# Scores and probabilities in joint runs of eight PSUM banks, and maxima that reach q by one transfer

## The chip, the cores and the metric

The kernel runs on one core of a Trainium2 chip. Five engines work side by side: PE (matmul), DVE (vector), ACT (activation), POOL (masks, some arithmetic) and SP, which issues the transfers. Matmul results land in eight PSUM banks of 128 partitions by 512 float32 columns; DVE and ACT read them out, and only then can a bank be written again. The metric is the device time of one execution in microseconds.

## The reference

A pre-norm transformer block over 2048 tokens of width 448: sliding-window attention with 16 heads of width 28 (each query sees itself and the 255 tokens before it), then a gated feed-forward of width 1792, each added to its input.

```python
q, k, v = qkv[0], qkv[1], qkv[2]
scores = jnp.einsum("bhqd,bhkd->bhqk", q, k) * (Dh ** -0.5)
mask = (idx[:, None] - idx[None, :] >= 0) & (idx[:, None] - idx[None, :] < W)
scores = jnp.where(mask[None, None], scores, -1e9)
p = _softmax(scores, axis=-1)
o = jnp.einsum("bhqk,bhkd->bhqd", p, v)
...
h = x + _A_ref(_layernorm(x, axis=-1), A_wqkv, A_wo)
h2 = h + _B_ref(_layernorm(h, axis=-1), B_w_gate, B_w_up, B_w_down)
```

`_B_ref` is `(gelu(x @ w_gate) * (x @ w_up)) @ w_down`.

## The kernel before

The kernel is a recorder and a planner. `block_kernel` calls `op` for each piece of work with an engine, an estimated duration, a key (the order wished for), the tokens it reads and writes and the PSUM banks it holds. `Lists.run` then lays all pieces out in one go with its own clock: for each engine it takes, among those that could start soonest, the one with the least key, picks banks for it through `allowed(kind)`, and emits its instructions. The result is a fixed order per engine. `TURN` is what the planner charges when PE changes its tile form (`mode`), `WAKE` what it charges for a signal between engines.

Attention is cut into 16 blocks `B`: four groups of four heads (`g = B % 4`) by four chunks of 512 queries (`c = B // 4`). In a block the queries are eight units of 64 and the keys of the window are units of 64 too. PE works in three tile forms here. Projections, values and the output product use the full 128 x 128 array (mode 0). Scores and probabilities use tiles of 32 rows by 64 columns (mode 3): `j` is the head and picks the 32 rows and the PSUM bank, `h` the half of the partitions. The value sums of `attend` use 64 x 32 (mode 2). The feed-forward uses halves of the array (mode 1).

The softmax goes in two passes. First the scores with queries along the partitions: DVE adds the mask and takes the maximum of each row (L783, an operation with a second small row that reads the result out). The maxima of a block are turned by DVE (L827), written to DRAM by four transfers (L829) and read back into the 29th row of q by one (L831). Second the products are made again with keys along the partitions, this time with 29 rows, so that the maximum is subtracted in the matmul; ACT takes the exponential into `pp` (L789), POOL zeroes what the mask excludes (L814), and `attend` multiplies with v (L882). A block has 16 score units for B under 4 and 20 after that, and as many probability units.

`scores_and_probs` makes one run of mode 3. It holds four banks, one for each `j`, and puts into each up to 512 columns: a score tile of a later block beside probabilities of an earlier one. So the two readers of a bank, DVE and ACT, take turns on it (`ser`). DVE throws the masked scores into `junk`, of which there are two, by `j % 2`. `stage(s)` lists the runs of a block: five for B from 4 on, four or three before.

The full-array work between the runs is q and k projection (`project_tile`, L659, copies to SBUF by ACT or DVE), values (`values`, L626) and the output product (`output`, L944, added to the residual by DVE, L947). `drain` brings the value sums out (ACT, then DVE L919 to L925 with POOL between).

## Time and profile before

| what | us |
|---|---|
| median of two runs | 712.58 |
| lowest and highest run | 711.46, 713.7 |
| the profiled execution | 712.76 |
| its span, first to last instruction | 710.9 |
| granted PE clock, mean | 0.995 |

The page gives each engine's busy time over the span. A busy PE is not a PE at its peak: the ends of matmuls are modelled, and a run that waits for a bank in its middle can still look busy. So the rows of the order of time are read by their starts: from the start of one stretch of a tile form to the start of the next is what the stretch held PE for. Each float32 matmul of modes 2 and 3 stands in the trace as two records. Names in rows are those of the program: `bank` is PSUM, `mt` the tile that holds mask and junk, `mx` the maxima, `pp` the probabilities.

### The profile page before, as it was taken

Reading aid. Unit: us, or ns where it says so; the run is one execution under the profiler, and the core shown is the slowest. Engines: PE = TensorE matmul, PEld = TensorE weight load, DVE = VectorE, ACT = ScalarE, POOL = GpSimd, SP = SyncE. Lnnn points to the kernel's source line nnn. Section 1 sums busy time; section 2 is a strip of 40 time slices with the busy share of each in tenths; the row PEclk is TensorE's granted clock in tenths of the full one; section 3 lists DMA queues with packets and bytes.
Section 4 is the critical chain, followed back from the end, with each engine's and each line's share of the span. In section 5 each row is a group of like instructions: output and inputs, shape, how many; then the busy total and the mean of one; then the engine's idle time right before and its main releaser. Section 6 shows DMA issues by size and latency. Waiting matters only on the chain. (4 is left out here: it accounts for less than half of the span.)

```text
span 710.9 us, 22675 instructions
## 1 busy us (share of the span) xinstructions
PE 692.3 (97%) x9106; PEld 566.4 (80%) x9106; DVE 535.9 (75%) x1409; ACT 361.0 (51%) x864; POOL 205.4 (29%) x430
## 2 busy tenths in 40 slices
PE   9999999999999989899999999999999999999997
PEld 7777667667776767576988897888888999999886
DVE  8977777877686668554997989975855888977744
ACT  5736536565455454455763547444434445545430
POOL 6334545564556345554020112000000110120000
PEclk9999999999999999899999999999999999999999
DMA  9211102022131226503745585424303564353102
GB/s 314 84 38 30 35 18 68 9 41 50 34 77 31 50 91 181 156 3 106 164 109 135 157 229 161 124 80 136 91 3 110 163 194 124 119 156 100 41 14 104
DMA packets 68744, 69.82 MB, mean 98 GB/s; under 512 B 44384, under 2 KB 56608, under 8 KB 68064
## 3 DMA queue, kind: packets, MB, share of 16 engines
q1 hardware_dynamic: 68496, 68.27, 34.5%
q8 instruction: 71, 1.16, 0.7%
q14 instruction: 33, 0.27, 0.1%
q10 hardware_dynamic: 144, 0.11, 0.0%
HBM read 58.95 MB, written 22.58 MB: 115 GB/s over the span
## 5 line engine op out<-in xcount | busy, mean ns | idle before, releaser
L783 DVE CUSTOM_DVE_ANT_0 mt<-bank,mt 128x320 bf16<-128x320 f32 (+4 forms) x288 | 122.8, 448 | 33.9 <-PE bank L773 18.5
L789 ACT ACTIVATE pp<-bank 128x192 f32<-128x192 f32 (+3 forms) x300 | 99.6, 390 | 75.7 <-PE bank L773 49.3
L1393 PE MATMUL bank<-xT,proj 64*128 64x512 f32 x645 | 120.1, 388 | 0.0
L814 POOL TENSOR_SCALAR_AFFINE_SELECT pp<-pp 64x256 f32<-64x256 f32 x240 | 96.3, 416 | 60.1 <-ACT pp L789 53.0
L1393 PE MATMUL bank<-xo,proj 64*128 64x512 f32 x456 | 97.3, 388 | 0.3 <-DVE e L1309 0.3
L659 PE MATMUL bank<-xT 128*128 128x512 f32 x308 | 83.8, 405 | 5.0 <-ACT pp L789 3.4
L1393 PEld LDWEIGHTS bank<-xT,proj 64*128 64x128 f32 x645 | 81.7, 184 | 7.7
L1469 PE MATMUL bank<-proj,gh 64*128 64x448 f32 x624 | 74.6, 362 | 0.4 <-DVE e L1309 0.4
L659 PEld LDWEIGHTS bank<-xT 128*128 128x128 f32 x308 | 55.1, 188 | 24.8 <-issue 7.9
L1469 PEld LDWEIGHTS bank<-proj,gh 64*128 64x128 f32 x624 | 62.6, 184 | 6.2 <-DVE e L1309 0.7
L1393 PEld LDWEIGHTS bank<-xo,proj 64*128 64x128 f32 x456 | 59.5, 184 | 6.9 <-DVE e L1309 0.7
L773 PE MATMUL bank<-q,k 29*64 29x128 f32 (+4 forms) x1888 | 61.3, 309 | 1.1 <-DVE mx L783 0.6
L773 PE MATMUL bank<-k,q 28*64 28x320 f32 (+4 forms) x1120 | 57.3, 410 | 0.7 <-ACT pp L789 0.6
L1393 PE MATMUL bank<-xT,w 64*128 64x512 f32 x276 | 53.5, 389 | 0.3 <-DVE raw L1405 0.3
L773 PEld LDWEIGHTS bank<-q,k 29*64 29x64 f32 x1888 | 40.6, 131 | 16.3 <-issue 3.2
L1393 PE MATMUL bank<-xo,w 64*128 64x512 f32 x240 | 49.4, 390 | 0.7 <-DVE raw L1405 0.6
L1488 DVE TENSOR_TENSOR hres<-bank,hres 128x448 f32<-128x448 f32 (+1 forms) x85 | 47.0, 610 | 1.0 <-PE bank L1469 1.0
L626 PE MATMUL bank<-proj,xT 128*128 128x448 f32 (+1 forms) x220 | 46.1, 339 | 0.1
L626 PEld LDWEIGHTS bank<-proj,xT 128*128 128x128 f32 x220 | 35.4, 189 | 7.7 <-issue 3.9
L882 PE MATMUL bank<-pp,v 64*29 64x128 f32 (+4 forms) x1888 | 40.7, 312 | 0.5 <-POOL pp L814 0.3
L882 PEld LDWEIGHTS bank<-pp,v 64*29 64x29 f32 x1888 | 34.2, 106 | 8.5 <-issue 3.7
L773 PEld LDWEIGHTS bank<-k,q 28*64 28x64 f32 x1120 | 23.1, 130 | 21.0 <-ACT pp L789 8.6
(195 smaller groups left out, 1278.6 us busy)
## 6 DMA issues: line engine op xcount, KB each, us to landing
gu<-in_gu_dram SPq DMA_DIRECT2D x18, 480.0 KB
proj<-gu SPq DMA_DIRECT2D x24, 288.0 KB
proj<-down SPq DMA_DIRECT2D x22, 224.0 KB
proj<-gu SPq DMA_DIRECT2D x24, 192.0 KB
hres<-in_x_dram SPq DMA_DIRECT2D x16, 224.0 KB
w<-gu SPq DMA_DIRECT2D x12, 288.0 KB
out_dram<-hres SPq DMA_DIRECT2D x15, 224.0 KB
xT<-xn SPq DMA_DIRECT2D x26, 128.0 KB
```

What stands on the lines that cost most here:

```text
L626: op("pe", mm(224 * n), 0.29 if n == 1 else 0.38, key + a / 16, lambda a=a, h=h, wb=wb, xb=xb: nc.tensor.matmul(bank[b.k][:, 0:224 * n], x ...
L659: op("pe", mm(512) + 0.002, 0.403, key, lambda a=a, h=h, wb=wb, xb=xb: nc.tensor.matmul(bank[b.k], wqk[m][:, h, wb, :], xT[:, xb, cc * 128 ...
L773: nc.tensor.matmul(bank[banks[j].k][dst, at:at + 64 * n], w, x, start=True, stop=True, tile_position=(32 * j, 64 * h), skip_group_check=True)
L783: nc.vector.tensor_tensor_reduce(junk[j % 2][hs, lo:320], bank[b.k][hs, o:o + n], mask[hs, lo:320], 1.0, -BIG, OP.add, OP.max, mx[u][hs, 4 ...
L789: op("act", 0.065 + G.w * 0.00088, 0.16 + G.w * 0.00088, key, lambda: nc.scalar.activation(pp[:, j, G.at:G.at + G.w], bank[b.k][:, o:o + G ...
L814: nc.gpsimd.affine_select(a, a, pattern=[[0, 4], [-cm, 64]], compare_op=op_, fill=0.0, base=0, channel_multiplier=cm)
L882: nc.tensor.matmul(bank[banks[h].k][32 * j:32 * j + DH + 1, 64 * lo:64 * hi], v[HALF[h], at_v(4 * c - 2 + kh // 2), 4 * g + j, :], pp[HALF ...
L1393: nc.tensor.matmul(bank[b.k], w, xarea(u.cp, xl, xs, side)[:, xk], start=p in (1, 2, 5) and not k and not t, stop=t == 2, tile_position=(6 ...
L1469: nc.tensor.matmul(bank[banks[q].k][:, 0:D], h[oh][0]()[HALF[x], q * 128:q * 128 + 128], d[wh][0]()[HALF[x]], start=not ph and not y and n ...
L1488: op("dve", 0.07 + w * 0.463 / D, 0.163 + w * 0.463 / D, key, lambda: nc.vector.tensor_tensor(hres[:, t, c0:c0 + w], bank[b.k][:, c0:c0 + ...
```

## The change

The score units of all blocks are laid end to end and cut into fills of eight (`filled`), 512 columns, and so are the probability units, with no regard to the borders of tiles or blocks. There are 38 fills of each. Excursion `e` makes the probabilities of fill `e - 4` in four banks and then, forced to follow at once (`then`), the scores of fill `e` in four others. So a run of mode 3 holds eight banks; the planner lets the last four come free late by the length of the first half (`soft`). From excursion 32 on the two halves are separate runs. A score tile may be cut at a bank: its maxima then come in two pieces, in columns 0 to 15 and 16 to 31 of `mx`, and DVE merges them (L877). The exponentials of a bank are one instruction (L853). `junk` is a single tile now; its second place and another hold the turned maxima, which DVE makes with four 32 x 32 transposes (L880), and four transfers bring them straight into q (L883). The planner charges more for a change of tile form (`TURN`), starts joint runs at least `GAP` apart, keeps value sums back for `AFTER` behind a run, takes them by a later key (`LAG_V`), and lets projections use all eight banks (`allowed`).

```diff
-LAG_V = 33.0
+LAG_V = 45.0
...
-TURN = (0.11, 0.11, 0.11, 0.11)
+TURN = (0.2, 0.2, 0.14, 0.16)
+HOLD = 0.3
+SPLIT = 32
+AFTER = 2.5
+GAP = 4.0
+LAG = 4
...
                     if not ks:
                         return None, None
-                    k = min(ks, key=lambda k: max(t, bank_free[k] + WAKE[e]))
-                    t = max(t, bank_free[k] + WAKE[e])
+                    late = o.soft if o.soft and i > 3 else 0
+                    k = min(ks, key=lambda k: max(t, bank_free[k] + WAKE[e] - late))
+                    t = max(t, bank_free[k] + WAKE[e] - late)
...
+            found, now = [], cand[e]
+            if e == "pe" and forced:
+                now = forced
+            elif e == "pe":
+                due = min((o.key for o in now if o.soft and max(o.ready, since + GAP) <= free["pe"] + HOLD), default=None)
+                if due is not None:
+                    now = [o for o in now if o.key <= due or all(b.k is not None for b in o.banks)]
+            for o in now:
                 t, got = start_of(e, o)
+                if t is not None and e == "pe" and o.mode == 2:
+                    t = max(t, since + AFTER)
...
-    junk = [mt[:, 192 + 192 * i:384 + 192 * i].bitcast(BF) for i in range(2)]
+    junk = mt[:, 192:352].bitcast(BF)
+    mxT = [mt[:, 352:480], mt[:, 576:704]]
...
+    def filled(items):
+        out, room = [[]], 8
+        for x, n in items:
+            a = 0
+            while a < n:
+                if not room:
+                    out.append([])
+                    room = 8
+                w = min(n - a, room)
+                out[-1].append((x, a, w, 8 - room))
+                a, room = a + w, room - w
+        return out
...
+    score_fills = filled([((B, i), max(tile_keys(B, i)[1])) for B in range(NB) for i in range(4)])
+    prob_fills = filled([((B, x), PIECES[x][4]) for B in range(NB) for x in
+                         ("ABdf" if B < 4 else "ABDFCE" if B % 2 == 0 else "CEABDF")])
+    final = {(B, i): (n, a) for n, fl in enumerate(score_fills) for (B, i), a, w, o in fl}
+    cut_tiles = {B: [i for i in range(4) if final[B, i][1]] for B in range(NB)}
+    scores_end = {B: final[B, 3][0] for B in range(NB)}
+    probs_end = {B: n for n, fl in enumerate(prob_fills) for (B, x), a, w, o in fl}
...
+        steps, new = [], []
+        if pf is not None:
+            work, reads, width, writes = [], [], 0, []
+            for (B, x), a, w, o in prob_fills[pf]:
+                reads += [("q", B % 4), *(("qx", B % 4, j) for j in range(4)), *k_toks(B, True)]
+                at = 512 * (pf % 4) + 64 * o
+                G = Group(B, [(piece_part(x, a, w), 0)], at)
+                groups.setdefault(B, []).append(G)
+                new.append(G)
+                writes += G.span(0, 64 * w)
+                ke, ko, ue, uo, n = piece_part(x, a, w)
+                for j in range(4):
+                    for h, kh, u in ((0, ke, ue), (1, ko, uo)):
+                        work += part(B, h, j, kh, u, n, 64 * o, True)
+                width = 64 * (o + w)
+            steps.append((work, reads, writes, width, [Bank("bin") for j in range(4)]))
...
+        ops = []
+        for n, (work, reads, writes, width, banks) in enumerate(steps):
+            held, rd, wr = banks, reads, writes
+            if not n and len(steps) > 1:
+                held, rd = banks + steps[1][4], reads + steps[1][1]
+            cost = width * 4 / 2400 + 0.012
+            ops.append(op("pe", cost, cost + 0.2, key, lambda work=work, banks=banks: run(work, banks), rd, wr, held, tag="bin", mode=3))
+        if len(ops) > 1:
+            L.open["whole"] = L.open.get("whole", 0) + 1
+            L.all.setdefault("whole", []).append(ops[0])
+            ops[0].then, ops[0].soft = ops[1], ops[0].cost
+        if sf is not None:
+            banks = steps[-1][4]
+            for j in range(4):
+                for (B, i), a, w, o in score_fills[sf]:
+                    most(key, B, i, a, w, o, j, banks[j])
+        if pf is not None:
+            width, banks = steps[0][3:]
+            for j in range(4):
+                probs(key, pf, width, j, banks[j])
+            for G in new:
+                select(G, key + 1)
...
-        def most(B, i, o, n, j, hs, b):
-            n, lo = 64 * n, 320 - 64 * n
-
-            def go():
-                u = B % 2
-                nc.vector.tensor_tensor_reduce(junk[j % 2][hs, lo:320], bank[b.k][hs, o:o + n], mask[hs, lo:320],
-                                               1.0, -BIG, OP.add, OP.max, mx[u][hs, 4 * j + i:4 * j + i + 1])
-            op("dve", 0.08 + n * 0.00104, 0.165 + n * 0.00106, key, go, ["mask"],
-               [("mx", B % 2, 4 * j + i, hs.start) if hs.stop - hs.start == 64 else ("mx", B % 2, 4 * j + i), *ser(b)], b, tag="most")
...
+    def most(key, B, i, a, w, o, j, b):
+        n, u = tile_keys(B, i)[1], B % 2
+        to = 4 * j + i + (16 if a else 0)
+        for h in (2,) if n[0] == n[1] else (0, 1):
+            full, hs = n[h % 2], HALF[h]
+            x = 64 * min(w, full - a)
+            lo = 320 - 64 * full + 64 * a
+
+            def go(hs=hs, x=x, lo=lo):
+                nc.vector.tensor_tensor_reduce(junk[hs, 0:x], bank[b.k][hs, 64 * o:64 * o + x], mask[hs, lo:lo + x],
+                                               1.0, -BIG, OP.add, OP.max, mx[u][hs, to:to + 1])
+            op("dve", 0.08 + x * 0.00104, 0.165 + x * 0.00106, key, go, ["mask"],
+               [("mx", u, to, h)] if h < 2 else [("mx", u, to)], b, tag="most")
...
+    def probs(key, pf, width, j, b):
+        at = 512 * (pf % 4)
+        op("act", 0.065 + width * 0.00088, 0.16 + width * 0.00088, key, lambda: nc.scalar.activation(
+            pp[:, j, at:at + width], bank[b.k][:, 0:width], AF.Exp, scale=SCALE), (), [span("pp", PW * j + at, width)], b, tag="exp")
...
-        op("dve", 0.1, 0.2, key, lambda: nc.vector.transpose(mxT[u], mx[u]), al, [("mxT", u)], port=True)
+        cuts = cut_tiles[B]
+        if cuts:
+            al += [("mx", u, 16 + 4 * j + i) for j in range(4) for i in cuts]
+            a, d = cuts[0], (cuts[1] - cuts[0] if len(cuts) > 1 else 1)
+            m2 = [mx[u][:, o:o + 16].rearrange("p (j i) -> p j i", i=4)[:, :, a:a + d * (len(cuts) - 1) + 1:d] for o in (0, 16)]
+            op("dve", 0.08, 0.165, key, lambda: nc.vector.tensor_tensor(m2[0], m2[0], m2[1], op=OP.max), al,
+               [("mx", u, 4 * j + i) for j in range(4) for i in cuts])
         for a in range(4):
-            dma(key, 2, lambda a=a: nc.sync.dma_start(mx_d[u][0:16, 32 * a:32 * a + 32], mxT[u][32 * a:32 * a + 16]), [("mxT", u)],
-                [("mxd", u, a)], cost=0.45)
-        dma(key, 8, lambda: nc.sync.dma_start(qT[g][DH:128:32], mx_d[u][0:16].rearrange("(j i) t -> j (i t)", i=4)),
-            [("mxd", u, a) for a in range(4)], [("qx", g)], cost=0.45)
+            op("dve", 0.07, 0.16, key, lambda a=a: nc.vector.transpose(mxT[u][0:32, 32 * a:32 * a + 32], mx[u][32 * a:32 * a + 32]),
+               al, [("mxT", u, a)], port=True)
+        for j in range(4):
+            dma(key, 4, lambda j=j: nc.sync.dma_start(
+                qT[g][32 * j + DH:32 * j + DH + 1].rearrange("p (i t) -> p i t", i=4), mxT[u][4 * j:4 * j + 4, None]),
+                [("mxT", u, a) for a in range(4)], [("qx", g, j)], cost=0.45)
...
+        last = scores_end[s] if s < NB else len(prob_fills) - 1 + LAG
+        while made_exc[0] <= last:
+            e = made_exc[0]
+            made_exc[0] += 1
+            sf, pf = e if e < len(score_fills) else None, e - LAG if LAG <= e < LAG + len(prob_fills) else None
+            key = 8 * e if e < 8 else 64 + 6.4 * (e - 8)
+            for x in ((sf, pf),) if e < SPLIT else ((None, pf), (sf, None)):
+                if x != (None, None):
+                    excursion(key, *x)
+            for B in range(NB):
+                if scores_end[B] == e:
+                    maxima(B)
+                if probs_end[B] == pf:
+                    collect(B)
...
         if kind in ("ln1", "v", "proj", "task"):
-            return [7, 6, 5, 4] + ([3, 2, 1, 0] if not left["bin"] or kind in ("v", "ln1") and L.fresh("bin") else [])
+            return [7, 6, 5, 4, 3, 2, 1, 0]
```

The fence below shows PE in the program before, behind a value sum: two runs with full-array work between. `k_158,q_162` are scores of one block, `q_165,k_161` probabilities of another; both go to the same four banks.

```order
L944 MATMUL bank_151<-wos,proj 128x448
L773 MATMUL bank_144<-k_158,q_162 64x320 x2
L773 MATMUL bank_145<-k_158,q_162 64x320 x2
L773 MATMUL bank_146<-k_158,q_162 64x320 x2
L773 MATMUL bank_149<-k_158,q_162 64x320 x2
L773 MATMUL bank_144<-q_165,k_161 64x192 x2
L773 MATMUL bank_145<-q_165,k_161 64x192 x2
L773 MATMUL bank_146<-q_165,k_161 64x192 x2
L773 MATMUL bank_149<-q_165,k_161 64x192 x2
L659 MATMUL bank_150<-xT 128x512 x3
L659 MATMUL bank_151<-xT 128x512 x6
```

And PE in the changed program, at the scores of block 7: the end of one run, one projection tile, and the first half of the next run. The names `k_157,q_161` are scores of block 7, `q_160,k_156` probabilities of block 6. Runs follow each other this closely in ten places.

```order
L784 MATMUL bank_145<-k_157,q_161 64x128 x2
L784 MATMUL bank_146<-k_157,q_161 64x128 x2
L784 MATMUL bank_147<-k_157,q_161 64x128 x2
L784 MATMUL bank_141<-k_157,q_161 64x128 x2
L680 MATMUL bank_140<-xT 128x512 x11
L784 MATMUL bank_142<-q_160,k_156 64x320 x2
L784 MATMUL bank_143<-q_160,k_156 64x320 x2
L784 MATMUL bank_144<-q_160,k_156 64x320 x2
L784 MATMUL bank_145<-q_160,k_156 64x320 x2
L784 MATMUL bank_142<-q_160,k_156 64x192 x2
L784 MATMUL bank_143<-q_160,k_156 64x192 x2
L784 MATMUL bank_144<-q_160,k_156 64x192 x2
```

Scores and probabilities no longer share a bank, and what stood as four banks of mixed work is eight banks of unmixed work; bank 145, written last by the first run, is wanted again in the next.

DVE before, two runs of scores one behind the other (`ISA mt,mx` is the reduction, `ISA mx` its read-out; the brackets name the engines that a row waits for):

```order
L783 ISA mt,mx_80<-bank_146,mt 128x320 [waits PE_49]
L783 ISA mx_80 128x1
L783 ISA mt,mx_80<-bank_150,mt 128x320 [waits DVE_49,PE_49]
L783 ISA mx_80 128x1
L783 ISA mt,mx_80<-bank_147,mt 128x320 [waits Activation_49]
L783 ISA mx_80 128x1
L783 ISA mt,mx_80<-bank_151,mt 128x320 [waits DVE_49,Activation_49]
L783 ISA mx_80 128x1
```

DVE in the changed program, the end of a run whose banks hold pieces of two blocks, and the maxima of the first of them:

```order
L846 ISA mt,mx_79<-bank_147,mt 128x256 [waits DVE_49,PE_49]
L846 ISA mx_79 128x1
L846 ISA mt,mx_80<-bank_147,mt 128x256 [waits DVE_49]
L846 ISA mx_80 128x1
L846 ISA mt,mx_79<-bank_140,mt 128x256 [waits DVE_49,PE_49,Activation_49]
L846 ISA mx_79 128x1
L846 ISA mt,mx_80<-bank_140,mt 128x256 [waits DVE_49]
L846 ISA mx_80 128x1
L877 TENSOR_TENSOR mx_79<-mx_79 128x8
L880 STREAM_TRANSPOSE mt<-mx_79 32x32 [waits DVE_49]
L880 STREAM_TRANSPOSE mt<-mx_79 32x32 x3
```

Every reduction here waits for an earlier DVE instruction, where every second one did; the waits for ACT on a shared bank are gone.

More of the change, by code (lines that the diff above doesn't have):

```diff
@@ L193, in start_of @@
             got = []
-            for b in o.banks:
+            for i, b in enumerate(o.banks):
                 if b.k is None:
@@ L260, in run @@
                 self.open[o.tag] -= 1
+            if o.then:
+                self.open["whole"] -= 1
             n -= 1
@@ L651, in project_tile @@
         main, extra = (("k", g, c % 2), ("kx", g, c % 2)) if s else (("q", g), ("qx", g))
+        more = [("qx", g, j) for j in range(4)] * (not s)
         B = 4 * c + g
@@ new lines, in excursion @@
+        if sf is not None:
+            work, reads, width = [], [], 0
+            for (B, i), a, w, o in score_fills[sf]:
+                g, c = block(B)
+                reads += [("q", g), *k_toks(B, False)]
+                lows, n = tile_keys(B, i)
+                for j in range(4):
+                    for h in range(2):
+                        work += part(B, h, j, lows[h] + a, 2 * i + h, min(w, n[h] - a), 64 * o, False)
+                width = 64 * (o + w)
+            steps.append((work, reads, [], width, [Bank("bin") for j in range(4)]))
@@ L1703, in block_kernel @@
             ln2(1)
-        make_groups(B)
         stage(B)
@@ L1750, in allowed @@
         if kind[0] == "gu0":
-            return [] if left["proj"] or left["v"] else [5 + kind[1]]
+            return [] if left["proj"] or left["v"] or left["whole"] else [5 + kind[1]]
         if kind[0] == "gu":
```

130 lines of the change are left out of this document (32 added, 98 removed).

## The prediction

> **What bounds the kernel now.** I read the page first, then the table of busy time by stretches, then the order of time on PE and DVE inside one stretch. The page says which engine has no room, the stretches say where the change can act.
>
> ```profile
> PE 692.3 (97%) x9106; PEld 566.4 (80%) x9106; DVE 535.9 (75%) x1409; ACT 361.0 (51%) x864; POOL 205.4 (29%) x430
> ...
> core 0: us, PE busy (x) PEld busy (x) DVE busy (x) ACT busy (x) POOL busy (x), PEclk, DMA share, GB/s
> 2.00:27.00 25.00, 24.66 (x142) 21.34 (x141) 22.23 (x54) 16.43 (x31) 14.96 (x37) 1.00 0.73 250
> 27.00:85.00 58.00, 56.21 (x849) 41.00 (x847) 46.62 (x220) 30.17 (x73) 21.89 (x45) 1.00 0.17 41
> 85.00:306.00 221.00, 213.50 (x4309) 154.05 (x4299) 162.21 (x534) 118.54 (x316) 116.85 (x264) 0.98 0.26 66
> 306.00:340.00 34.00, 32.85 (x534) 24.68 (x518) 16.31 (x31) 19.35 (x47) 15.72 (x37) 1.00 0.17 57
> 340.00:708.00 368.00, 364.65 (x3304) 325.05 (x3303) 287.58 (x570) 176.47 (x400) 34.70 (x43) 1.00 0.43 120
> ```
>
> Attention runs from 27 to 340 us; from 340 on PE does the feed-forward matmuls, busy 364.65 of 368 us, in the same number and tile forms before and after the change. So only the first 340 us can move. PE is the bound there, but its 97% hides three things: columns, changes of tile form, and short waits. The second engine matters: from 85 to 306 us, the twelve blocks 4 to 15, DVE is busy 162.21 of 221 us.
>
> **The price of leaving the full-array form.** These rows give it by differences.
>
> ```profile
> 27.41 0.79 PE L773 MATMUL bank<-k,q 28*64 28x320 f32 x16
> 28.13 2.60 PE L626 MATMUL bank<-proj,xT 128*128 128x224 f32 x21
> ...
> 178.28 2.81 PE L659 MATMUL bank<-xT 128*128 128x512 f32 x11
> 181.03 2.56 PE L882 MATMUL bank<-pp,v 64*29 64x192 f32 x128
> ...
> 238.38 0.73 PE L659 MATMUL bank<-xT 128*128 128x512 f32 x2
> 239.04 2.56 PE L882 MATMUL bank<-pp,v 64*29 64x192 f32 x128
> 241.53 0.79 PE L773 MATMUL bank<-k,q 28*64 28x320 f32 x16
> 242.12 0.53 PE L773 MATMUL bank<-q,k 29*64 29x192 f32 x16
> 242.58 0.50 PE L659 MATMUL bank<-xT 128*128 128x512 f32 x1
> ```
>
> A run of 16 x 320 = 5120 recorded columns holds PE 0.72 us (27.41 to 28.13), one of 8192 columns 1.05 us (241.53 to 242.58). 3072 more columns cost 0.33 us, so 5120 cost 0.55, and 0.17 to 0.18 us per run is left that is no column. In the same way two full-array matmuls hold PE 0.66 us, eleven 2.75: 0.23 each, and 0.20 per stretch that is none of them. A trip out and back costs 0.38 us.
>
> In the order of the two programs PE goes from 70 stretches of score form to 45, and from 74 full-array stretches to 55 (value sums keep 16): 25 x 0.18 + 19 x 0.20 = **8.3 us less**. This lies on PE, which sets the end, so nothing hides it.
>
> The columns are the same. The matmuls are cut otherwise: score form goes from 1504 to 1612 (two records each, so 216 more), value sums from 944 to 832 (224 records fewer).
>
> ```profile
> 153.80 1.20 PE L773 MATMUL bank<-q,k 29*64 29x128 f32 x48
> 154.93 1.42 PE L659 MATMUL bank<-xT 128*128 128x512 f32 x5
> ```
>
> These 8192 columns in 48 records take 1.13 us where 32 records took 1.05, 5 ns a record: +1.1 and -1.1, so 0, at worst 1 us either way.
>
> **What DVE gets in exchange.** A score tile that crosses a bank is reduced in two pieces: 400 reductions at L846 for 288 at L783. All of them now write one scratch tile, where two took turns. In the program 363 of the 400 wait for an earlier DVE instruction, of the 288 it was 152. What such a wait costs can be read here; the small row behind each reduction reads its result out.
>
> ```profile
> 187.10 0.49 DVE L783 CUSTOM_DVE_ANT_0 mt<-bank,mt 128x320 bf16<-128x320 f32 x1 [1.00 <-PE bank L773]
> 187.52 0.08 DVE L783 DVE_READ_ACCUMULATOR2_ANT mx<- 128x1 f32 x1
> 187.75 0.49 DVE L783 CUSTOM_DVE_ANT_0 mt<-bank,mt 128x320 bf16<-128x320 f32 x1
> 188.16 0.08 DVE L783 DVE_READ_ACCUMULATOR2_ANT mx<- 128x1 f32 x1
> 188.16 0.48 DVE L783 CUSTOM_DVE_ANT_0 mt<-bank,mt 128x320 bf16<-128x320 f32 x1
> ...
> 191.70 0.08 DVE L783 DVE_READ_ACCUMULATOR2_ANT mx<- 128x1 f32 x1
> 191.82 0.21 DVE L827 STREAM_TRANSPOSE mxT<-mx 128x32 f32<-128x32 f32 x1
> ...
> L783 DVE CUSTOM_DVE_ANT_0 mt<-bank,mt 128x320 bf16<-128x320 f32 x224 | 104.0, 484 | 28.2 <-PE bank L773 13.9 <-ACT pp L789 1.0 <-DVE mx L783 1.0
> L783 DVE CUSTOM_DVE_ANT_0 mt<-bank,mt 64x64 bf16<-64x64 f32 x16 | 3.3, 215 | 5.0 <-PE bank L773 4.6 <-ACT pp L789 0.2
> ```
>
> The reduction at 188.16 has no such wait and starts together with the read-out before it, 0.41 us behind its forerunner. The one at 187.75 waits for its own engine and for another one, and starts 0.65 behind: 0.23 lost. The transpose at 191.82 waits for its own engine alone and starts 0.04 after the read-out has ended instead of together with it: 0.12 lost. By width a column costs (484 - 215) / 256 = 1.05 ns, and 0.08 us is fixed.
>
> A bank of 512 score columns comes in 2.4 pieces on average: 0.54 + 2.4 x 0.08 + 0.23 (its first piece also waits for PE) + 1.4 x 0.12 = 1.13 us, 4.5 us for the four banks of a run. A block of blocks 4 to 15 is two and a half runs, 11.3 us. Before it was 16 reductions at 0.41 plus 0.23 for 58% of them, 8.7 us. Four small transposes for one and a merge of split maxima cost 0.1 to 1.0 us a block (the 0.21 row above is the nearest, the pieces are a quarter of it; I take 0.3), and copies of q and k that go from DVE to ACT give 0.25 back. So DVE gains 2.6 us of work per block, 31 us between 85 and 306. Its free time there is 221 - 162 = 59 us, less 0.14 us behind some 110 read-outs that no row counts as busy: 43. It is left with 12 us, and fewer if PE is to be faster.
>
> **What this does to PE.** Before, a run that stood directly behind another already waited for banks:
>
> ```profile
> 185.98 0.79 PE L773 MATMUL bank<-k,q 28*64 28x320 f32 x16
> 186.57 0.53 PE L773 MATMUL bank<-q,k 29*64 29x192 f32 x16
> 186.89 0.74 PE L773 MATMUL bank<-k,q 28*64 28x320 f32 x16
> 187.43 1.02 PE L773 MATMUL bank<-q,k 29*64 29x192 f32 x20
> 188.66 0.48 PE L773 MATMUL bank<-q,k 29*64 29x128 f32 x8 [0.21 <-ACT pp L789]
> 189.73 1.10 PE L773 MATMUL bank<-q,k 29*64 29x128 f32 x36 [0.58 <-DVE mx L783]
> 190.76 0.47 PE L944 MATMUL bank<-proj,ohl 128*128 128x448 f32 x1
> ```
>
> Its 24576 columns need 2.6 + 0.2 us and took 4.78: 2.0 lost. The same subtraction over all stretches from 27 to 340 leaves 29 us of waits, 12 of them in the seven stretches of this kind.
>
> After, a run takes all eight banks. Walk one that is followed by one projection tile of 11 matmuls, as in the order shown above. The run starts at 0, its scores are there at 2.0. PE reaches the next run at 2.0 + 2.75 = 4.75 and its score half at 5.6. ACT has emptied the probabilities long before,
>
> ```profile
> 287.05 2.06 ACT L789 ACTIVATE pp<-bank 128x512 f32<-128x512 f32 x4 [0.53 <-PE bank L773]
> ```
>
> four banks in 2.06 us. But DVE empties the score banks at 3.2, 4.4, 5.7 and 6.9, and the score half needs the last of them for its first eight matmuls: 1.35 us lost. Ten gaps are this short: 13.5 us. One run stands directly behind another: some 4 us. In the 18 longer gaps DVE has 6 to 12 us and I put 0.2 us each, 3.5. Together 21 us in place of 12: **9 us more**. The bounds: nothing (or the 12 us saved) if DVE keeps up, 38 us if each of the 28 joint runs loses 1.35.
>
> **The rest.** The maxima reach q without the hop through DRAM, four DMAs in place of five on SP's queue.
>
> ```profile
> 154.29 2.15 SPq L829 DMA_DIRECT2D mx<-mxT  x4
> ...
> 159.39 0.50 SPq L831 DMA_DIRECT2D q<-mx  x1
> ...
> PE bank L773 <- DMA q<-mx: 0.2, 1, 0.2
> ```
>
> The first hop took 5 us, yet PE waited for these maxima 0.2 us in all, so this gains nothing; at least one whole run still lies between a block's last scores and its first probabilities. ACT does 152 exponentials for 300, 6 to 15 us less, and five more copies; it was idle nearly half the stretch, so that is worth 0. POOL masks the same 240 pieces. The value sums come later; if they came too late, the four slots of probabilities would block ACT, and at 118.54 busy of 221 it has room.
>
> **Sum.** The profiled execution took 712.76 us, a span of 710.9 and 1.9 around it; the median of the runs is 712.58. 712.8 - 8.3 + 0 + 9 = 713.5, and I say **714**.
>
> **Rivals.** *The waits inside DVE hide* (704). If DVE's own waits cost nothing, its work grows only by 112 x 0.08 = 9 us, the 43 us of free time cover it, waits stay at 29 us, and 712.8 - 8.3 = 704.5. For it: DVE is 75% busy overall. Against it: 0.65 against 0.41 in the rows above. The Trainium skill, page "VectorE: DVE Perf Modes", section "The DRAIN you can't avoid", says that a semaphore between chained DVE operations costs nothing extra, which gives this rival. The trace disagrees: an operation without a wait starts 0.12 to 0.23 us sooner.
>
> *Eight banks cure the ends of the blocks* (693). The 12 us of waits in stretches of runs behind runs go, and no new ones come: 712.8 - 8.3 - 12. Against it: there is one such stretch left, and the score half now needs all of the banks DVE empties.
>
> *DVE paces every run* (731). If the free 12 us are not where they are needed, each of 28 joint runs loses 1.35 us: 38 in place of 12, 712.8 - 8.3 + 26. It decides once DVE's other work (value drains, residual adds, norms: 13.5 us busy a block less 7.5 for reductions, 6) is queued ahead of the score banks in the long gaps too. For it: the planner still counts a reduction at 0.08 us and 1.04 ns a column, without own waits, so its order takes DVE to be early.
>
> **Numbers.** About 2% (14 us) is what a measurement of this kernel tells from no change: under 698.3 is faster, over 726.8 slower. The forecast has 0.50, hidden waits 0.28, the cure 0.10, DVE at every run 0.12. So faster 0.10, same 0.78, slower 0.12. The range leaves the last two out: 702 to 727. The forecast's own range is 708 to 722.
>
> **What would show it.** Right: 45 score stretches, each joint run near 1.9 us of columns; reductions 0.12 or 0.23 us behind the read-out before them; DVE above 80% busy from 85 us to the end of the scores; PE's waits for L846 at the short gaps above 1 us. Wrong: waits of PE on DVE below 10 us in all, feed-forward starting 8 us earlier (then 704), or a second half of each run that waits everywhere. It would also be wrong if the step from probabilities to scores inside a run pays the 0.18 us again: 28 x 0.18 = 5 us more.

## The result: slower, and where the time went

The changed kernel takes 735.2 us (median of two runs, 734.4 to 736.0) where the kernel before takes 712.6: a ratio of 1.032 with a 95% interval from 1.023 to 1.040. The prediction said 714 and a range from 702 to 727.

From the page of the changed kernel: busy time of the engines, PE's granted clock in 40 slices, and the reductions and exponentials by line (busy us, mean ns | idle before, and its releaser).

```profile
PE 701.2 (95%) x9098; PEld 578.5 (79%) x9098; DVE 570.2 (78%) x1688; ACT 349.3 (48%) x723; POOL 208.1 (28%) x432
...
PEclk9988899999999999999999999999999999999999
...
L846 DVE CUSTOM_DVE_ANT_0 mt<-bank,mt 128x320 bf16<-128x320 f32 (+6 forms) x400 | 147.8, 369 | 47.7 <-PE bank L784 23.1
L853 ACT ACTIVATE pp<-bank 128x512 f32<-128x512 f32 x152 | 78.7, 600 | 44.8 <-PE bank L784 44.8
```

DVE is busy 34 us longer than before, ACT 12 us less, and PE's clock dips soon after the start of attention, where it was full before. The table by stretches shows the phase in which the time is lost; the last row is the feed-forward part, moved by 24 us.

```profile
27.00:85.00 58.00, 51.86 (x695) 39.18 (x693) 48.71 (x238) 24.60 (x47) 17.55 (x36) 0.88 0.13 35
85.00:306.00 221.00, 206.46 (x3958) 155.64 (x3962) 177.46 (x725) 103.50 (x195) 105.96 (x238) 0.97 0.23 59
...
364.00:732.00 368.00, 363.99 (x3303) 322.59 (x3300) 285.70 (x567) 176.42 (x399) 38.19 (x45) 1.00 0.43 121
```

Feed-forward is as long as before (363.99 busy of 368, 364.65 before). All of the loss lies ahead of it: between 27 and 85 us PE does 695 matmuls where it did 849, at a clock of 0.88 where it was 1.00. PE's waits between 27 and 345 us (us in all, times, longest) name who is late:

```profile
PE bank L784 <- DVE mx L846: 12.1, 17, 2.1
PE bank L646 <- DVE mx L846: 2.9, 2, 2.5
...
PEld bank L784 <- DVE mx L846: 23.1, 33, 2.5
```

Before, the same views had 0.6 us and 2.7 us in these places:

```profile
PE bank L773 <- DVE mx L783: 0.6, 1, 0.6
...
PEld bank L773 <- DVE mx L783: 2.7, 7, 0.8
```

One gap in the order of time, a joint run behind eleven projection matmuls:

```profile
121.85 1.12 PE L784 MATMUL bank<-q,k 29*64 29x320 f32 x32
122.77 1.12 PE L784 MATMUL bank<-k,q 28*64 28x192 f32 x12
124.61 1.08 PE L784 MATMUL bank<-k,q 28*64 28x192 f32 x20 [0.72 <-DVE mx L846]
125.62 1.08 PE L646 MATMUL bank<-proj,xT 128*128 128x448 f32 x4
```

The run holds PE 3.77 us for 16384 columns that need 1.9: the probabilities pass, the scores stand until DVE has emptied the banks. And this is why DVE is late, in the same stretch (DVE):

```profile
119.48 0.49 DVE L846 CUSTOM_DVE_ANT_0 mt<-bank,mt 128x320 bf16<-128x320 f32 x1
119.89 0.08 DVE L846 DVE_READ_ACCUMULATOR2_ANT mx<- 128x1 f32 x1
120.01 0.29 DVE L846 CUSTOM_DVE_ANT_0 mt<-bank,mt 128x128 bf16<-128x128 f32 x1
```

Each reduction starts 0.04 us after the read-out ahead of it has ended, not together with it. That much was foreseen. What the experiments had to say was whether it is the cause, and why it costs more than forecast.

### The profile page after: what moved, and what is told of

Its sections match the earlier page's. It is cut to its first block, busy times and chain, and to the rows that moved or that the text cites. A ratio compares the mean times of both kernels' runs of the same rounds, so it can differ in the third digit from the quotient of the medians.

```text
span 734.3 us, 22776 instructions
## 1 busy us (share of the span) xinstructions
PE 701.2 (95%) x9098; PEld 578.5 (79%) x9098; DVE 570.2 (78%) x1688; ACT 349.3 (48%) x723; POOL 208.1 (28%) x432
## 5 line engine op out<-in xcount | busy, mean ns | idle before, releaser
L846 DVE CUSTOM_DVE_ANT_0 mt<-bank,mt 128x320 bf16<-128x320 f32 (+6 forms) x400 | 147.8, 369 | 47.7 <-PE bank L784 23.1
L853 ACT ACTIVATE pp<-bank 128x512 f32<-128x512 f32 x152 | 78.7, 600 | 44.8 <-PE bank L784 44.8
L680 PE MATMUL bank<-xT 128*128 128x512 f32 x308 | 86.5, 425 | 0.7 <-DVE mx L846 0.5
L680 PEld LDWEIGHTS bank<-xT 128*128 128x128 f32 x308 | 59.5, 202 | 18.9 <-issue 3.1
L784 PE MATMUL bank<-k,q 28*64 28x320 f32 (+4 forms) x1560 | 59.4, 348 | 14.3 <-DVE mx L846 11.6
L784 PEld LDWEIGHTS bank<-k,q 28*64 28x64 f32 x1560 | 38.9, 134 | 27.4 <-DVE mx L846 19.0
L784 PE MATMUL bank<-q,k 29*64 29x192 f32 (+4 forms) x1664 | 48.4, 334 | 0.7 <-DVE mx L846 0.5
L784 PEld LDWEIGHTS bank<-q,k 29*64 29x64 f32 x1664 | 32.3, 134 | 19.0 <-issue 6.1
L646 PEld LDWEIGHTS bank<-proj,xT 128*128 128x128 f32 x220 | 38.0, 202 | 11.3 <-DVE mx L846 4.2
L932 PE MATMUL bank<-pp,v 64*29 64x192 f32 (+4 forms) x1664 | 39.8, 319 | 0.7 <-DVE mx L846 0.7
```

Source lines behind the costliest of these rows:

```text
L646: op("pe", mm(224 * n), 0.29 if n == 1 else 0.38, key + a / 16, lambda a=a, h=h, wb=wb, xb=xb: nc.tensor.matmul(bank[b.k][:, 0:224 * n], x ...
L680: op("pe", mm(512) + 0.002, 0.403, key, lambda a=a, h=h, wb=wb, xb=xb: nc.tensor.matmul(bank[b.k], wqk[m][:, h, wb, :], xT[:, xb, cc * 128 ...
L784: nc.tensor.matmul(bank[banks[j].k][dst, at:at + 64 * n], w, x, start=True, stop=True, tile_position=(32 * j, 64 * h), skip_group_check=True)
L846: nc.vector.tensor_tensor_reduce(junk[hs, 0:x], bank[b.k][hs, 64 * o:64 * o + x], mask[hs, lo:lo + x], 1.0, -BIG, OP.add, OP.max, mx[u][hs ...
L853: op("act", 0.065 + width * 0.00088, 0.16 + width * 0.00088, key, lambda: nc.scalar.activation(pp[:, j, at:at + width], bank[b.k][:, 0:wid ...
L932: nc.tensor.matmul(bank[banks[h].k][32 * j:32 * j + DH + 1, 64 * lo:64 * hi], v[HALF[h], at_v(4 * c - 2 + kh // 2), 4 * g + j, :], pp[HALF ...
```

## Experiments

Three theories stood at the start. Theory 1: the waits of reductions on the one just ahead, through the single scratch tile, make DVE late. Rival 1: joint runs, which need eight banks, are the trouble by themselves. Rival 2: the planner's order, made for a reduction of 0.08 us and 1.04 ns a column, is wrong. Medians are in us; each ratio, with its 95% interval, is to the kernel before, measured along with it on the same chip. The kernel before took 712.6 to 715.7 us on these occasions, so a difference between medians taken on different ones is good to some 3 us.

### The waits, taken away and added

The scratch tile becomes a strip in which a reduction seldom writes where the last one did.

```diff
-junk = mt[:, 192:352].bitcast(BF)
+junk = mt[:, 192:512].bitcast(BF)    # place(x): next x columns, up to 640 and back down
...
-tensor_tensor_reduce(junk[hs, 0:x], ...
+y = place(x)
+tensor_tensor_reduce(junk[hs, y:y + x], ...
```

The tiles that lay behind the scratch (`mxT`, `kept`) move to make room, here and in the runs with two scratch tiles.

> The changed kernel with its one scratch tile for the masked scores made 640 columns wide and used as a strip that is walked up and back down, so that a reduction seldom writes where the one just before it wrote: 140 of the 400 reductions wait for an earlier VectorE instruction in place of 363 (before the change 152 of 288). The order of all engines is the same. Theory 1 (the own waits make VectorE late, and late reductions hold the eight banks that a joint run needs): 223 waits fewer at 0.12 to 0.23 us are 27 to 51 us of VectorE time less; the short gaps ahead of the full-array stretches (9 of 1.1 to 2.7 us) and part of the loss in the first four blocks go, 735 becomes 712 to 722. Rival 1 (eight banks at a time are the trouble, whoever reads them): VectorE's busy time falls, the stretches keep their length, 731 to 736. Rival 2 (the planner's order is wrong for the new runs): 728 to 735, since the order is the same.

Measured: 709.6, ratio 0.994 [0.992, 0.996]. 25.6 us are gone with 223 waits, 0.115 us each, with PE's stretches in the same order. The time is even below the range of theory 1. Rival 1 and rival 2 can't hold the bulk.

The opposite, in the kernel before: `junk[j % 2]` becomes `junk[0]`.

> The kernel before with one scratch tile in place of two: 251 of its 288 reductions wait for an earlier VectorE instruction, 152 before. Nothing else differs. Theory 1: 99 waits more at 0.12 to 0.23 us are 12 to 23 us of VectorE time, and 712.6 becomes 716 to 726, in the early blocks above all. Rival 1 (eight banks at a time): no effect without joint runs, 711 to 715.

Measured: 726.2, ratio 1.017 [1.014, 1.020]. 99 waits more cost 13 us, without any joint run. In the groups by line the row of the reductions reads so (before: 122.8 busy, mean 448 ns, 33.9 idle):

```profile
L783 DVE CUSTOM_DVE_ANT_0 mt<-bank,mt 128x320 bf16<-128x320 f32 (+4 forms) x288 | 129.8, 451 | 44.2 <-PE bank L773 17.9
```

One reduction is as long as it was (451 against 448 ns), but fewer overlap the read-out before them, 7 us of busy time more, and DVE stands 10 us longer ahead of them. The estimate was 12 to 23 us.

Then two scratch tiles used in turn. Nearly as many waits stand in the program as with one tile, but for the last reduction but one.

```diff
-junk = mt[:, 192:352].bitcast(BF)
+junk = [mt[:, 192 + 160 * i:352 + 160 * i].bitcast(BF) for i in range(2)]
...
-tensor_tensor_reduce(junk[hs, 0:x], ...
+jturn[0] += 1
+tensor_tensor_reduce(junk[jturn[0] % 2][hs, 0:x], ...
```

> The changed kernel with two scratch tiles used in turn, so that a reduction writes where the last but one wrote: 346 of 400 reductions still wait for an earlier VectorE instruction (363 with one tile, 140 with the strip), but nearly all for one that is an instruction further back. If what costs 0.12 us is that the reduction just before it must have ended (its last results written) ahead of the next one's start, the cost goes with the strip's and the time is 708 to 714. If any wait on the engine's own work costs it, wherever what it waits for stands, 730 to 736.

Measured: 704.9, ratio 0.987 [0.983, 0.991], somewhat below the first range. So it isn't the wait as such. DVE's rows in this kernel, at the place shown above:

```profile
109.47 0.49 DVE L848 CUSTOM_DVE_ANT_0 mt<-bank,mt 128x320 bf16<-128x320 f32 x1
109.88 0.08 DVE L848 DVE_READ_ACCUMULATOR2_ANT mx<- 128x1 f32 x1
109.88 0.29 DVE L848 CUSTOM_DVE_ANT_0 mt<-bank,mt 128x128 bf16<-128x128 f32 x1
```

0.41 from start to start where it was 0.53. Over all neighbours that don't wait for PE, the median at 128x320 is 0.534 in the changed kernel, 0.411 here with the wait and 0.413 without. And PE, the run shown above:

```profile
112.15 1.12 PE L785 MATMUL bank<-q,k 29*64 29x320 f32 x32
113.07 1.24 PE L785 MATMUL bank<-k,q 28*64 28x192 f32 x32
114.24 1.28 PE L647 MATMUL bank<-proj,xT 128*128 128x448 f32 x5
```

2.09 us in place of 3.77. Between 85 and 306 us PE is now busy 216.68 of 221, at full clock:

```profile
85.00:306.00 221.00, 216.68 (x4523) 169.19 (x4523) 173.42 (x781) 114.77 (x219) 124.76 (x284) 1.00 0.26 66
```

### Where the waits cost

Since the order is the same, the two traces can be laid side by side, stretch by stretch of one tile form. What each stretch holds PE longer with the waits (start to start, from the rows of PE):

```
                                            waits    in turn   longer
stretches up to 102.5 us                                         8.6
run at 121.85                               3.77      2.09       1.7
run at 148.71                               3.56      1.91       1.7
... nine such runs behind a short gap in all                    12.1
double run at 171.60                        7.49      6.16       1.3
full-array stretches at 102.56, 132.51, 179.09,
  211.25, 275.38, 295.41, 331.54                                 6.9
the rest, mostly after 280 us                                    3.9
all                                                             32.8
```

Two runs divide it: scratch in turn for the reductions of blocks 0 to 3 alone (`jturn[0] += B < 4`), and for the others alone (`B > 3`).

> The changed kernel with two scratch tiles used in turn by the reductions of blocks 0 to 3 alone; those of blocks 4 to 15 keep one tile and their waits. Going by the two traces set side by side (same order, one with waits, one in turn), the changed kernel is 10 to 11 us behind by the value sum of block 3 and 33 by the last: if the losses add, 722 to 727. If a late start is made up for later, or the other way round sets the rest (the first blocks alone decide), 731 to 736 or 705 to 712.

Measured: 728.2, ratio 1.019 [1.016, 1.022].

> The mirror of the run before: blocks 0 to 3 keep one scratch tile and its waits, blocks 4 to 15 use two in turn. If the losses add, the first blocks' 10 to 11 us stay: 713 to 718. If the first blocks' delay is absorbed later, 705 to 710.

Measured: 710.7, ratio 0.995 [0.993, 0.997]. Set against 735.2, the first blocks give 7.0 us and the others 24.5, together 31.5 where both at once give 30.3. Each time lies between the two ranges that were set for it, but the losses add, within what such differences are good for. Of the 8 to 11 us that the first blocks are behind in the side-by-side, 6 to 7 are left at the end: a little of an early delay is made up for.

### The planner told the truth

```diff
-op("dve", 0.08 + x * 0.00104, 0.165 + ...
+op("dve", 0.2 + x * 0.00104, 0.285 + ...
```

> The changed kernel, one scratch tile and all its waits kept, with the planner told what a waiting reduction takes (0.20 us and 1.04 ns a column in place of 0.08 and 1.04 ns, as the trace of the changed kernel shows: 0.268 us at 64 columns, 0.534 at 320), planned anew. If the loss is the planner's (an order made for a faster VectorE), 712 to 722. If it is VectorE's time itself, 728 to 738.

Measured: 726.4, ratio 1.016 [1.012, 1.021]. That lies between the two ranges: some 9 of the 30 us that the waits cost come back with an order that knows of them, and two thirds stay, with DVE's time itself as what is left to explain them.

### Joint runs

`SPLIT = 0` issues both halves of every joint run apart, `8 <= e < SPLIT` those of the first eight fills. First with the waits in place:

> The changed kernel with the two halves of every joint run issued as runs of their own (probabilities of one fill, scores of another, four banks each), planned anew; fills, pieces, scratch tile and the maxima's path stay as changed. Rival 1 (eight banks at a time are the trouble): the waits of the first four blocks and the short gaps go, and some 25 more form changes come back at 0.18 us each, 715 to 722. Theory 1 (own waits): VectorE is as late as it was, and only the wait for all eight banks turns into shorter ones: 726 to 736.

> The changed kernel with joint runs only from the ninth fill on, so that the first four blocks issue scores and probabilities apart; planned anew. If joint runs are the cause of the 20 us that the first four blocks lost, 715 to 722. If VectorE's longer reductions and more pieces are the cause there, 728 to 736.

Measured: 743.3, ratio 1.040 [1.037, 1.043], and 732.3, ratio 1.026 [1.022, 1.029]. The first lies above both of its ranges. Then without the waits, by the strip and by scratch in turn:

> The changed kernel with the strip (709.6 us), and every joint run issued as two runs of four banks, planned anew. If joint runs are worth what the change of form costs on TensorE (some 25 full-array stretches and as many runs more, at about 0.19 us each), 713 to 719. If eight banks at a time hold VectorE and ScalarE up as much as that, 706 to 712.

> The changed kernel with two scratch tiles in turn, and joint runs only from the ninth fill on (the first four blocks issue scores and probabilities apart), planned anew. With the waits gone the first four blocks still end 5 us later than before the change. If joint runs are why, 699 to 703. If it is the fills cut into five pieces (28 reductions a block where there were 24, and a block's first scores waiting for its neighbour's), 704 to 708.

Measured: 719.9, ratio 1.007 [1.004, 1.009], and 701.6, ratio 0.982 [0.979, 0.985]. Joint runs are worth 8 to 10 us whether DVE waits or not; rival 1 falls. In the first four blocks alone, leaving them out gains some 3 us, no more than a new order can do by itself (below). The last kernel has the lowest median of all and beats both kernels, the one before by 1.8%.

### The kernel before, with its own waits taken

> The kernel before with its two scratch tiles made one strip of 768 columns that is walked up and down: 105 of 288 reductions wait for an earlier VectorE instruction (152 before), and 38 (74 before) for that and a second engine. If the own waits cost what they cost in the changed kernel, 36 double waits at 0.22 us and 11 single ones at 0.12 are 9 us of VectorE time less, and the time falls to 706 to 711; then most of what the strip gained over the kernel before is the strip's own. If VectorE isn't late enough in the kernel before for it to matter, 711 to 714.

> The kernel before with its two scratch tiles used strictly in turn (before, the tile went by the bank's number, so that two reductions of one bank, or of the first and third, wrote the same one). If waits on the reduction just before cost the kernel before time as they cost the changed one, it gains what their number gives: of 152 own waits some 49 stand with a second wait, 0.22 us each, 11 us of VectorE time, and 704 to 710 follow; then the change with scratch in turn (704.9) is worth little against it. If VectorE has the time to spare there, as the strip showed (715), 711 to 716, and the change with scratch in turn is worth 7 to 10 us.

Measured: 715.4, ratio 1.001 [0.999, 1.004], and 710.8, ratio 0.993 [0.990, 0.996]. Little or nothing: before the change DVE had time for its waits. Adding 99 costs 13 us (above), taking the existing ones gains nothing with the strip and 5 us in turn. The kernel before had the room for most of the waits that it had, and none for 99 more. With scratch in turn on both sides the change is worth some 6 us (704.9 against 710.8).

### The steps that were taken at nothing

On top of scratch in turn, the maxima by two hops through DRAM as before the change, and then the old list of banks.

```diff
-for a in range(4): transpose(mxT[u][0:32, 32*a:32*a+32], mx[u][32*a:32*a+32])
-for j in range(4): dma(qT[g][32*j+DH], mxT[u][4*j:4*j+4])
+transpose(mxT[u], mx[u])
+for a in range(4): dma(mx_d[u][0:16, 32*a:32*a+32], mxT[u][32*a:32*a+16])
+dma(qT[g][DH:128:32], mx_d[u][0:16])
```

> The changed kernel with two scratch tiles in turn (704.9 us), and the maxima's way as before the change: one transpose of 128 rows, four DMAs to DRAM, one DMA from there to q; planned anew. If the maxima come early enough either way, as the prediction took it (the hop is worth 0): 703 to 708. If the second hop, some 5 us, makes the first probabilities of a block late: 709 to 720.

```diff
-return [7, 6, 5, 4, 3, 2, 1, 0]
+return [7, 6, 5, 4] + ([3, 2, 1, 0] if not left["bin"] or ... else [])
```

> The changed kernel with two scratch tiles in turn (704.9 us), and the old list of banks: projections, values and transposes take banks 4 to 7 only, the others once the scores are done; planned anew. If the list matters little: 703 to 709. If projections in banks 0 to 3 hold up runs that need all eight, the old list is faster, 698 to 702; if projections lack banks under it, 710 to 730.

Measured: 717.2, ratio 1.005 [1.002, 1.008], and 724.1, ratio 1.015 [1.011, 1.020]. Both are dear, and both orders are new. How much a new order costs by itself can be seen when the planner's prices hardly differ:

> The changed kernel with two scratch tiles in turn (704.9 us), and the planner's four prices for a change of form 0.01 us higher; nothing else differs but the order that follows from it. If a new plan as such costs little: 702 to 708, and the 12 us of the two hops are the hops'. If plans differ by 5 to 20 us by chance, this one is 708 to 722.

> The changed kernel with two scratch tiles in turn (704.9 us), and the planner's price for a score reduction 0.005 us higher; nothing else differs but the order. The same two theories: 702 to 708, or 708 to 722.

> The run with the two hops (717.2 us), and the planner's four prices for a change of form 0.01 us higher. If the hops cost 12 us whatever the plan: 713 to 721. If that plan was an unlucky one: 703 to 711.

Measured: 702.2 (ratio 0.982 [0.979, 0.985]), 708.3 (0.991 [0.989, 0.994]), and with two hops 719.2 (1.006 [1.003, 1.008]). New orders of the same kernel lie 3 us to either side, so 1 to 3 us between replanned kernels (the first blocks' 3 us above among them) show nothing; the two hops cost 9 to 17, in two orders. Both orders show the same wait. DVE, in the first of the two:

```profile
161.54 0.25 DVE L973 RECIPROCAL rcp<-oblk 128x16 f32<-128x16 f32 x1
165.30 0.65 DVE L539 STREAM_TRANSPOSE xn<-xn 128x448 f32<-128x448 f32 x1 [3.51 <-DMA xn<-xn]
165.87 0.45 DVE L849 CUSTOM_DVE_ANT_0 mt<-bank,mt 128x320 bf16<-128x320 f32 x1
```

DVE waits 3.51 us for rows of the layer norm with a run's reductions behind them, and PE then stands 5.15 us for reductions. In the second order the same instruction waits 3.88 us. With one hop no such wait is among the largest of DVE. Why these rows come late isn't shown. A suspect is SP's queue, in which the second hop (L886) stands until the first has landed, 7.5 us in all between 27 and 345 us; but the kernel before, where PE waited 0.2 us for maxima, has such a row too (L831):

```profile
SPq L886 <- DMA mx<-mt: 7.5, 7, 1.7
...
SPq L831 <- DMA mx<-mxT: 7.8, 5, 2.6
```

And at the place above the second hop hardly stands; it follows 0.17 us behind the transfer ahead of it:

```profile
147.91 1.86 SPq L692 DMA_DIRECT2D k<-k  x3
149.94 0.50 SPq L886 DMA_DIRECT2D q<-mx  x1
```

So the price of the two hops is measured, and its way to PE is followed from the late rows on, not up to them.

With the old bank list, PE's waits between 27 and 345 us begin with this row:

```profile
PE bank L681 <- DVE mx L848: 9.4, 9, 1.8
```

L681 are projection matmuls: confined to four banks, they wait for reductions, 0.2 us with the wide list. That is as much as half of the 19 us; the other half was not followed.

## Why the prediction was wrong, step by step

**The failed step is "Together 21 us in place of 12: 9 us more".** The other terms came out in sum, partly by luck (see the rest, below): without the waits the same order takes 704.9, and 712.8 - 8.3 was 704.5. The waits cost 30.3 us in place of 9, and 712.8 - 8.3 + 30.3 is 734.8, against 736.0 in the profiled execution. The same shows when the prediction's prices for columns, records and stretches are taken off what all stretches hold PE for, an estimate from PE's rows: some 27 us of waits are left before, 60 in the changed kernel and 27 with scratch in turn. Both halves of the step were off.

- *The 21 us.* The price of a wait was right: 0.12 us alone (0.534 against 0.413), 0.22 with a second engine's wait (0.637 against 0.417 in the kernel before). The places that the step names were nearly right: nine runs behind a short gap lose 12.1 us where ten were to lose 13.5, the double run 1.3 for 4, the rest 3.9 for 3.5. DVE was 80% busy between 85 and 306 us (177.46 of 221), as forecast. Two terms are missing. Blocks 0 to 3 cost 8.6 us by the table and 7.0 by the run; DVE's 43 us of free time were counted from 85 us on, and between 27 and 85 us it was 80% busy before the change already (46.62 of 58). And the full-array stretches behind late reductions are longer, 6.9 us.
- *The 12 us in return.* The waits of runs behind runs were taken as saved. No such gain is to be seen: even without own waits 27 us of waits are left, as before, and the kernel gains 7.7 us, no more than the form changes were to bring. The double run at 155.70 still holds PE 6.16 us for 4.2 of columns, records and one change of form, and the first four blocks still end later than before (value sum of block 3 at 115.5 us, 110.8 before).

The full-array stretches grow in two ways. Of their 6.9 us, 4.0 lie in four stretches (102.56, 132.51, 211.25 and 295.41) at a granted clock of 1.00 in both kernels: projections and output products, too, wait for banks that DVE has yet to read (their weight loads stand 3.3 us for reductions in these four). The other 2.9 us lie in three stretches where the clock falls: 179.09 at 0.81, 275.38 at 0.59, 331.54 at 0.69, all at 1.00 with scratch in turn. In the first blocks this is plainest. First the changed kernel, PE's rows and the row of the full-array stretch in the table by stretches (clock third from the end), then the same with scratch in turn:

```profile
82.88 0.54 PE L784 MATMUL bank<-k,q 28*64 28x192 f32 x8
84.76 0.54 PE L784 MATMUL bank<-k,q 28*64 28x192 f32 x4 [1.34 <-DVE mx L846]
86.68 1.97 PE L784 MATMUL bank<-k,q 28*64 28x192 f32 x20 [1.38 <-DVE mx L846]
88.58 5.03 PE L680 MATMUL bank<-xT 128*128 128x512 f32 x11
93.54 0.80 PE L784 MATMUL bank<-q,k 29*64 29x320 f32 x16
```

```profile
88.58:93.54 4.96, 4.96 (x13) 3.47 (x11) 3.87 (x19) 1.44 (x3) 3.07 (x7) 0.51 0.28 48
```

```profile
79.67 0.54 PE L785 MATMUL bank<-k,q 28*64 28x192 f32 x4 [0.86 <-DVE mx L848]
81.33 1.08 PE L785 MATMUL bank<-k,q 28*64 28x192 f32 x20 [1.11 <-DVE mx L848]
82.34 2.79 PE L681 MATMUL bank<-xT 128*128 128x512 f32 x11
85.06 1.12 PE L785 MATMUL bank<-q,k 29*64 29x320 f32 x32
85.97 1.07 PE L785 MATMUL bank<-k,q 28*64 28x320 f32 x32
86.97 0.50 PE L681 MATMUL bank<-xT 128*128 128x512 f32 x1
```

```profile
82.34:85.06 2.72, 2.72 (x14) 1.99 (x12) 2.72 (x16) 2.33 (x5) 2.22 (x4) 1.00 0.40 72
```

Two waits of 1.34 and 1.38 us, 0.75 longer together than those of the other kernel, and the eleven matmuls behind them run at a clock of 0.51 and take 4.96 us for 2.72; the twenty ahead of those take 1.90 for 1.01. The waits cost 0.75 us and what follows them 3.1. In all, the changed kernel's clock is at 0.50 for 30.7 us of attention (42.25 to 49.08, 55.91 to 62.73, 86.63 to 93.45, 178.79 to 182.20, 274.36 to 277.77 and 332.39 to 335.80), with scratch in turn for 3.4 (42.33 to 45.74). Half of the difference, 14 us, is the most that the clock can have in the 32.8; it is likely less, for the second run of the changed kernel, at a mean clock of 0.986 where the profiled one had 0.977 (a difference of 6.6 us over the span), took only 1.7 us less. This is read from the traces; no run changed the clock alone.

**The first blocks** were left out of the sum without a look at their pieces. The first fill of a block there has five pieces a bank, four of them 64 rows high. In the changed kernel:

```profile
45.37 0.29 DVE L846 CUSTOM_DVE_ANT_0 mt<-bank,mt 64x128 bf16<-64x128 f32 x1
45.59 0.08 DVE L846 DVE_READ_ACCUMULATOR2_ANT mx<- 64x1 f32 x1
45.70 0.35 DVE L846 CUSTOM_DVE_ANT_0 mt<-bank,mt 64x192 bf16<-64x192 f32 x1
```

and with scratch in turn:

```profile
43.71 0.29 DVE L848 CUSTOM_DVE_ANT_0 mt<-bank,mt 64x128 bf16<-64x128 f32 x1
43.93 0.08 DVE L848 DVE_READ_ACCUMULATOR2_ANT mx<- 64x1 f32 x1
44.04 0.35 DVE L848 CUSTOM_DVE_ANT_0 mt<-bank,mt 64x192 bf16<-64x192 f32 x1
```

0.33 us from start to start in both: these pieces start behind the read-out whatever the wait, so the repair doesn't help them. The kernel before has the same 64 pieces of 64 rows, but four of one kind stand in a row there, and most start together with the read-out:

```profile
45.22 0.29 DVE L783 CUSTOM_DVE_ANT_0 mt<-bank,mt 64x128 bf16<-64x128 f32 x1
45.45 0.08 DVE L783 DVE_READ_ACCUMULATOR2_ANT mx<- 64x1 f32 x1
45.45 0.29 DVE L783 CUSTOM_DVE_ANT_0 mt<-bank,mt 64x128 bf16<-64x128 f32 x1
```

At 0.11 us each, 64 such starts are up to 7 us of DVE's time (an estimate), which fits that the first blocks stay 5 us late; no run set the order of these pieces alone. The Trainium skill, page "VectorE: DVE Perf Modes", section "Two Vector instructions with no wait between them", says that an instruction whose input begins in another group of 32 rows than that of the last one to read the same memory starts only when all earlier ones have finished. The pieces of a bank alternate between rows 0 and 64, and the trace agrees: 0.33 us where the rows change, 0.23 where they stay.

**The rivals.** *The waits inside DVE hide*: as a statement on this kernel it is wrong, and its 704.5 is what the kernel takes once they are gone. The sentence of the Trainium skill it leaned on (page "VectorE: DVE Perf Modes", section "The DRAIN you can't avoid": the semaphore costs nothing extra) was measured there on copies; here it holds where the awaited instruction has ended (0.411 against 0.413 us) and not where it is the one just ahead (0.534). *DVE paces every run* gave 731 and came nearest, for a partly wrong reason: not every run loses 1.35 us, nine do, and the rest is the first blocks, the full-array stretches and the ends. *Eight banks cure the ends* has no support: the waits are 27 us before and with scratch in turn.

**The rest.** *The form changes* (8.3 us) are borne out by the count: PE's rows with scratch in turn have 45 stretches of score form for 70 and 21 full-array stretches fewer, where 19 were counted. The runs without joint halves bring only 18 and 10 of them back, some 5 us at the prediction's prices; the rest of their 8 to 10 us is waits and a new order. A joint run doesn't pay the step between its halves: 16384 columns that begin at 85.06 in the rows above end where the next stretch starts, at 86.97, 1.91 us. *The hop* was put at 0 because PE hardly waited for maxima; in the new arrangement it is worth 9 to 17 us. The bank list isn't a term of the sum at all, and is worth 19. That 704.9 still meets 704.5 is luck to that extent: something as large stands against the hop and the bank list, and which pieces of the new fills that is stays open.

## What to carry to other kernels

Give consecutive operations of one engine different places to write, even for output that nobody reads: two in turn were worth 30 us here, at no other change. When an engine has 43 us left over in a stretch and a change asks for 31 of it, the cost isn't what overflows: ask at which gaps it is late, and count the start of the program, where it was fullest, first. An edit that looks free by who waits for its result may still be dear: the second hop cost 9 to 17 us, though PE had waited 0.2 us in all for what it brings.

## What was not expected of the hardware

- A wait of DVE on its own work costs by its distance: 0.12 us on the reduction just ahead, nothing on the last but one.
- Two waits of PE of 1.3 to 1.4 us, some half a microsecond of work apart, were followed by 5 us at a granted clock of 0.51; waits of 0.86 and 1.11 at the same place by 1.00.
- Reductions of 64 rows that alternate between rows 0 and 64 start 0.11 us behind the read-out ahead of them, whether they wait for it or not; of the same rows, they can start together with it.
